# A fused channel-attention and two-FFN kernel: the order of DVE's work in the units of the first pair

## The chip, the cores and the metric

The kernel runs on one core of a Trainium2 chip. The metric is device time in microseconds (us) of one execution. Five engines are named: PE (TensorE, matrix products; its weight loads are shown as PEld), DVE (VectorE, element-wise work), ACT (ScalarE, activations and copies), POOL (GpSimd) and SP (SyncE, which issues transfers). Each engine has its own queue of instructions and works through it in order; semaphores tie the queues together.

## What is computed

The reference, cut to what matters (6016 tokens, 256 channels):

```python
qn = q / (norm(q over tokens) + 1e-6);  kn = k / (norm(k over tokens) + 1e-6)
a = softmax(kn^T @ qn / tau)                  # 256 x 256
x = v @ a                                     # tokens x 256
x = (silu(x @ w_gate) * (x @ w_val)) @ w_out  # 256 -> 1536 -> 256
h = x @ w_in                                  # 256 -> 2048
out = (h * clip(h + 3, 0, 6) / 6) @ w2_out    # 2048 -> 256
```

The five FFN weights arrive as 64-bit floats, and are seen by the kernel as pairs of 32-bit words (a low and a high word).

## The kernel before, in words

Attention is over channels, so its 256x256 matrix is formed once and folded into the first FFN's input weights (w_gate and w_val become a @ w_gate and a @ w_val). The tokens are then taken in pairs of blocks, block 0 and block 1 of 512 tokens each. Every product of two matrices is made as three matmuls, high by high, low weight by high data, high weight by low data: `mm3` (line 96 in the trace, L96).

**Jobs.** A weight block of 128x512 elements is turned from its two words into one float by a `Job`. Its DMA (L109, on SP) brings the raw words into one of two `raw` buffers. `fields()` calls four steps: `cut` on DVE takes out the exponent `e` (L117) and the mantissa bits `m` (L120), `power` on ACT turns `e` into a power of two with two activations (L127, L129), and `mantissa` (L133) and `sign` (L139) on DVE complete `m`. One unit later `scale()` on DVE multiplies the two (L152). For a gate or value block the result goes to `wf`, to be folded; for a block of w_out (a "back weight") ACT's `high()` (L156) copies it rounded into `wo`, and DVE's `low()` (L161) writes the rest.

**The first pair.** The first pair of blocks is worked off in 24 units while the weights are still being converted: one unit for each of 12 slices of 128 hidden channels and each of two blocks (only the last four are in another order). A unit issues, per engine in this order:
- PE: two products of 12 matmuls in all into two PSUM banks (gate first, then value); after units 1, 2, 5, 6, ... 17, 18 a fold of the next weight block (8 matmuls, L628); then the back product (`back`, 6 matmuls into `o`) of the unit whose h was split two units before. The banks b0, b1, a and d are taken in turn by products and folds, and a bank can be written again once its reader is done: Silu for the gate bank, the product on DVE for the value bank, the two copies L705 for a fold's bank.
- ACT: the high part of the last unit's h (L1024), Silu of the gate bank (L1048), `high()` if a w_out block is scaled in this unit, the two `power` activations if there are fields in this unit, and after a fold the two copies of its bank (L705) and the high part of the new weights (L712).
- DVE: the low part of the last unit's h (L1026), low parts of freshly folded weights (L717), `scale()`, the field steps, the product of Silu and value (L1059), `low()`, and what `beside` holds for the unit: sums of the weights (L181 to L184, units 3, 7, 11, 15, 17, 19), the low part of these sums (L717, 128x1024, units 8, 12, 16, 17, 20), and in units 18 to 21 the preparation of the next pair (L337, L340, L349).

The tables `fields` and `scaling` say in which units this happens. Fields: units 0, 1, 2, 4, 5, 6, 8, 9, 10, 12, 13, 14, 16, 17 and 19. Scaling is in the unit after each of these; it is that of a w_out block in units 2, 6, 10, 14, 18 and 20. Units 0, 4, 8, 12, 16 and 19 have fields but no scaling.

After the 24 units the other pairs follow as "cubes", seven products in place of eight (a Strassen scheme), and then the second FFN. The order is written out by hand: within `tc.manual_schedule()` each engine takes the instructions as the program emits them.

Of the kernel before, what the change touches and what calls it, by code (L numbers as in the profile page):

```python
# [18 lines left out]
def channel_attention_then_two_ffns(  # L19
# [71 lines left out]
    def mm3(out, w, x, start, stop):  # L91

        wh, wl = w
        xh, xl = x
        for w, x, first, last in ((wh, xh, start, False), (wl, xh, False, False), (wh, xl, False, stop)):
            nc.tensor.matmul(out, lhsT=w, rhs=x, start=first, stop=last, skip_group_check=True)  # L96
# [136 lines left out]
    jobs, at, second = [], {}, []  # L233
# [32 lines left out]
    passed = [0] * 4  # L266
    limit = [NJ1]

    def load_jobs(ahead=RAW):
        while passed[0] < min(limit[0], passed[1] + ahead):  # L270
            jobs[passed[0]].load()
            passed[0] += 1
# [160 lines left out]
    with tc.manual_schedule():  # L433
# [262 lines left out]
        def fold(m, g):  # L696

            ps = next_bank([P, CT, CW])
            for c in range(CT):
                folding(ps[:, c, :], m, g, c, c == 0)  # L700
            folded.add((m, g))
            fa = FA[g % 2]
            o = CT * m
            for c in range(CT):
                nc.scalar.activation(fa[:, (c, 3 - c)[m]], ps[:, c, :], AF.Copy, scale=rden[:, c : c + 1])  # L705

            w1_hi(g, o, fa[:, o : o + 2])
            return lambda: w1_lo(g, o, fa[:, o : o + 2])
# [27 lines left out]
        def next_bank(shape):  # L736
            tag = ("b0", "b1", "a", "d")[turn[0] % 4]
            turn[0] += 1
            return ps_f.tile(shape, F32, tag=tag, name="ps_" + tag[0])
# [4 lines left out]
        def h_tile(layer):  # L744
            i = counts["h"] = counts["h"] + 1
            if layer == 2 and i % 10 >= 5:
                if i % 10 < 8:
                    return tmp_p.tile([P, TB], F32, tag="m", name="h")
                return e_p.tile([P, TB], F32, tag="e", name="h")
            return h_p.tile([P, TB], F32, tag="h", name="h")  # L750
# [167 lines left out]
        def back():  # L918

            layer, p, block, f, hl = backs.pop(0)  # L920
            t0, n = pairs[p]
            nf = (NF1, NF2)[layer - 1]
            if layer == 1 and p == 0 and f % CT == 0 and block == 0:
                assert passed[3] > at["out", f // CT]
            if f == 0:
                accs[block] = [ps_acc.tile([P, TB], F32, tag=f"acc{CT * block + e}", name="o") for e in range(CT)]
            w = w_of(layer, f)
            for e in range(CT):
                mm3(
                    accs[block][e][:, :n],  # L930
                    (w[:, 0, e * P : (e + 1) * P], w[:, 1, e * P : (e + 1) * P]),
                    (hl[:, 0, :n], hl[:, 1, :n]),
                    f == 0,
                    f == nf - 1,
                )
            if f < nf - 1:
                return
            if (layer, p) not in xr:
                xr[layer, p] = xr_p.tile([P, 2, CT, TB], F32, tag="xr", name="xo")
            x = xr[layer, p]  # L940
            for e in range(CT):
                scale = 1.0 if layer == 1 else 1.0 / 6.0

                if e and p == NP - 1:
                    nc.vector.tensor_scalar(
                        out=x[:, block, e, :n], in0=accs[block][e][:, :n], scalar1=scale, scalar2=None, op0=ALU.mult
                    )
                else:
                    nc.scalar.activation(x[:, block, e, :n], accs[block][e][:, :n], AF.Copy, scale=scale)
                if layer == 1:  # L950
                    nc.sync.dma_start(out=x2_d[p][:, block, e, :n], in_=x[:, block, e, :n])
                else:
                    t = t0 + block * n
                    nc.sync.dma_start(out=outT[e * P : (e + 1) * P, t : t + n], in_=x[:, block, e, :n])
# [30 lines left out]
        fields, scaling, beside = {}, {}, {i: [] for i in U}  # L985
# [35 lines left out]
        def plain_split(between):  # L1021
            f, b, h = h_of
            hl = hl_tile(1)
            nc.scalar.activation(hl[:, 0, :n], h[:, :n], AF.Copy)  # L1024
            between()
            nc.vector.tensor_tensor(out=hl[:, 1, :n], in0=h[:, :n], in1=hl[:, 0, :n].bitcast(F32), op=ALU.subtract)  # L1026
            backs.append((1, 0, b, f, hl))

        for i, (f, b) in enumerate(units):
            w = w_in[1, f // 2][:, f % 2]  # L1030
            pss = []
            for row in ((A11, A12), (S1, A22)):
                ps = next_bank([P, TB])
                for k in range(CT):
                    x = v0[b, k]
                    mm3(
                        ps[:, :n],
                        (w[:, 0, row[k], :], w[:, 1, row[k], :]),
                        (x[:, 0, :n], x[:, 1, :n]),
                        k == 0,  # L1040
                        k == CT - 1,
                    )
                pss.append(ps)

            if h_of:
                plain_split(lambda: None)
            h = h_tile(1)
            nc.scalar.activation(h[:, :n], pss[0][:, :n], AF.Silu)  # L1048
            for go in lows:
                go()  # L1050
            lows = []
            if i in scaling:
                jobs[scaling[i]].scale()
                jobs[scaling[i]].high()
            if i in fields:
                jobs[fields[i]].fields()
                passed[1] += 1
                load_jobs()
            nc.vector.tensor_tensor(out=h[:, :n], in0=h[:, :n], in1=pss[1][:, :n], op=ALU.mult)  # L1059
            h_of = (f, b, h)  # L1060
            if i in scaling:
                jobs[scaling[i]].low()
                passed[2] = passed[3] = scaling[i] + 1
            if i == 10:
                d1, d2, d3, d4, d5, d6 = prep(1)
                for j, step in ((18, d1), (19, d2), (19, d3), (20, d4), (21, d5), (21, d6)):
                    beside[j].append(step)
            for step in beside[i]:
                step()
            g = i // 4 + 1  # L1070
            if i % 4 in (1, 2) and g < NG1:
                m = i % 4 - 1
                assert passed[2] > at[m, g]
                lows.append(fold(m, g))
            while len(backs) > LAG - 1:
                back()
# [5 lines left out]
        for c, key in enumerate(cubes):  # L1082
            layer, p, i = key
# [94 lines left out]
```

## Time and profile before

| what | value |
| --- | --- |
| median of 3 runs | 1103.3 us (1103.25 to 1105.0) |
| the profiled execution | 1105.07 us |
| its span, first to last instruction | 1103.2 us |
| mean granted TensorE clock | 0.999 |
| PE busy | 1090.3 us (99%) |
| PE weight loads busy | 916.2 us (83%) |
| DVE busy | 799.8 us (72%) |
| ACT busy | 760.1 us (69%) |
| POOL busy | 78.2 us (7%) |

The span runs from the first to the last instruction of the profiled execution; its own time is 1.87 us longer. Busy shares are averages over stages with different limits. Matmuls are pipelined and their ends are modelled, so a busy PE is not PE at its peak. In a timeline each row gives the start, the busy time (instructions merged into one row are counted behind the x), the engine, the line, the operation with out<-in, and in brackets the idle time of the engine just before it with what ended it. The busy times of neighbours on one engine overlap a little, so the step from one start to the next is what an operation costs its queue.

### The profile page before, as it was taken

The page shows a single profiled execution, that of the slowest core. Times are in us where ns is not written, and L with a number is a line of the kernel's source. Part 1 is how long each engine was busy: PE and PEld are TensorE (multiplying, and loading weights), DVE is VectorE, ACT ScalarE, POOL GpSimd, SP SyncE. Part 2 cuts the span into 40 slices and gives each one's busy share as a digit, 9 for nine tenths or more (in the row PEclk, how much of TensorE's full clock was granted, in tenths as well). Part 3 has the DMA queues.
Part 4 walks back from the last instruction along what each step waited for, and adds up shares of the span by engine and source line. Part 5 has one row for each costly group of instructions (what it writes and reads, how often), then busy time and mean ns, then how long its engine had stood idle before and what let it go on. Part 6 is the DMA issues. An engine that isn't in the chain of part 4 may idle for free.

```text
span 1103.2 us, 13706 instructions
## 1 busy us (share of the span) xinstructions
PE 1090.3 (99%) x4878; PEld 916.2 (83%) x4878; DVE 799.8 (72%) x1259; ACT 760.1 (69%) x1318; POOL 78.2 (7%) x92
## 2 busy tenths in 40 slices
PE   8989999999999999999999999999999999999998
PEld 6878888888888888888899888888888888888997
DVE  6888996776777677677676677687687687677665
ACT  6666656666766776666766677776766776776765
POOL 0000000111122121211210000000000000000000
PEclk9999999999999999999999999999999999999999
DMA  9523303136337325523665814314324224224100
GB/s 352 211 77 95 115 20 111 62 129 229 110 129 246 132 115 197 199 98 135 225 231 221 330 77 139 128 77 153 115 82 152 111 95 155 89 84 149 40 1 34
DMA packets 56324, 150.31 MB, mean 136 GB/s; under 512 B 5056, under 2 KB 17088, under 8 KB 54848
## 3 DMA queue, kind: packets, MB, share of 16 engines
q1 hardware_dynamic: 55824, 148.92, 37.8%
q8 instruction: 38, 0.62, 0.2%
q10 hardware_dynamic: 432, 0.52, 0.2%
q14 instruction: 30, 0.25, 0.1%
HBM read 89.78 MB, written 59.64 MB: 135 GB/s over the span
## 4 chain that ended last, share of the span: by engine, by line
PE 88%; DVE 6%; ACT 4%; issue 1%; DMA 1%; ACTq 0%; DVEq 0%
PE o L96 38%; PE ps_b L96 20%; PE ps_a L96 13%; PE ps_d L96 13%; PE s L554 4%; DVE hl L1026 1%; DVE w L717 1%; DVE h L1059 1%; ACT w L712 1%; ACT FA L705 1%; ACT hl L1024 1%; DMA tk<-in_k 1%; ACT e L129 1%; ACT e L127 0%; DVE m L133 0%
## 5 line engine op out<-in xcount | busy, mean ns | idle before, releaser
L855 DVE TENSOR_TENSOR hl<-h,hl 128x512 fp32r<-128x512 f32 (+1 forms) x312 | 210.0, 685 | 156.1 <-ACT hl L789 150.8
L96 PE MATMUL o<-hl,w2o 128*128 128x512 f32 (+1 forms) x1152 | 287.6, 385 | 0.0
L96 PEld LDWEIGHTS o<-hl,w2o 128*128 128x128 f32 x1152 | 215.9, 188 | 40.8 <-DVE hl L855 0.6
L789 ACT ACTIVATE hl<-h 128x512 fp32r<-128x512 f32 (+1 forms) x312 | 187.6, 617 | 56.9 <-DVE h L839 52.9
L96 PE MATMUL o<-hl,wo 128*128 128x512 f32 (+1 forms) x864 | 218.1, 387 | 2.1 <-DVE wo L161 1.3
L96 PEld LDWEIGHTS o<-hl,wo 128*128 128x128 f32 x864 | 162.0, 188 | 33.3 <-DVE wo L161 1.7
L96 PE MATMUL ps_b<-op,w 128*128 128x512 f32 (+1 forms) x540 | 139.6, 384 | 0.0
L96 PEld LDWEIGHTS ps_b<-op,w 128*128 128x128 f32 x540 | 101.3, 188 | 18.9 <-ACT ps_b L789 0.4
L96 PE MATMUL ps_b<-op,w2i 128*128 128x512 f32 (+1 forms) x432 | 112.0, 385 | 0.0
L793 DVE TENSOR_TENSOR h<-h,ps_d 128x512 f32<-128x512 f32 (+1 forms) x108 | 72.6, 672 | 52.4 <-PE ps_d L96 47.5
L789 ACT ACTIVATE h<-ps_b 128x512 f32<-128x512 f32 (+1 forms) x108 | 63.4, 587 | 66.7 <-PE ps_b L96 65.7
L789 ACT ACTIVATE ps_b<-ps_a 128x512 f32<-128x512 f32 (+1 forms) x108 | 61.9, 573 | 55.2 <-PE ps_a L96 55.2
L96 PE MATMUL ps_a<-op,w 128*128 128x512 f32 (+1 forms) x360 | 99.4, 384 | 0.0
L96 PE MATMUL ps_d<-op,w 128*128 128x512 f32 (+1 forms) x360 | 99.4, 384 | 0.0
L833 ACT ACTIVATE h<-h,three 128x512 f32<-128x512 f32 (+1 forms) x96 | 68.7, 716 | 40.8 <-DVE h L793 39.5
L96 PEld LDWEIGHTS ps_b<-op,w2i 128*128 128x128 f32 x432 | 81.1, 188 | 15.1
L96 PE MATMUL ps_d<-op,w2i 128*128 128x512 f32 (+1 forms) x288 | 79.8, 385 | 0.1
L793 DVE TENSOR_TENSOR h<-h,ps_b 128x512 f32<-128x512 f32 (+1 forms) x108 | 72.6, 672 | 10.0 <-PE ps_b L96 7.5
L96 PE MATMUL ps_a<-op,w2i 128*128 128x512 f32 (+1 forms) x288 | 79.8, 385 | 0.0
L96 PEld LDWEIGHTS ps_a<-op,w 128*128 128x128 f32 x360 | 67.6, 188 | 12.4
L96 PEld LDWEIGHTS ps_d<-op,w 128*128 128x128 f32 x360 | 67.6, 188 | 12.3
L839 DVE SCALAR_TENSOR_TENSOR h<-h 128x512 f32<-128x512 f32 (+1 forms) x96 | 65.0, 677 | 12.5 <-ACT h L833 12.5
(138 smaller groups left out, 1301.1 us busy)
## 6 DMA issues: line engine op xcount, KB each, us to landing
op<-opd SPq DMA_DIRECT2D x56, 512.0 KB, 4.8
opd<-sp SPq DMA_DIRECT2D x42, 512.0 KB, 2.7
raw<-in_moe_w_out SPq DMA_DIRECT2D x14, 512.0 KB, 4.3
w2i<-wi_d SPq DMA_DIRECT2D x4, 1792.0 KB, 7.4
opd<-st SPq DMA_DIRECT2D x14, 512.0 KB, 2.6
op<-opd SPq DMA_DIRECT2D x14, 448.0 KB, 4.1
tq<-in_q SPq DMA_DIRECT2D x14, 384.0 KB, 7.5
tk<-in_k SPq DMA_DIRECT2D x14, 384.0 KB, 7.5
```

What stands on the lines that cost most here:

```text
L96: nc.tensor.matmul(out, lhsT=w, rhs=x, start=first, stop=last, skip_group_check=True)
L129: nc.scalar.activation(e, e.bitcast(F32), AF.Relu, scale=-1.0, bias=exp_span)
L554: nc.tensor.matmul(s_ps[c], lhsT=tk[:, j - chunks[i][0], c * P : (c + 1) * P], rhs=tq[:, j - chunks[i][0], :], start=(j == 0), stop=(j == ...
L705: nc.scalar.activation(fa[:, (c, 3 - c)[m]], ps[:, c, :], AF.Copy, scale=rden[:, c : c + 1])
L712: nc.scalar.activation(hi, src.rearrange("p o (c f) -> p c o f", c=2), AF.Copy)
L717: nc.vector.tensor_tensor(out=lo, in0=src, in1=hi.bitcast(F32), op=ALU.subtract)
L789: nc.scalar.activation(out[:, : self.n], src[:, : self.n], AF.Copy)
L793: nc.vector.tensor_tensor(out=out[:, :n], in0=a[:, :n], in1=b[:, :n], op=ALU.add)
L833: nc.scalar.activation(r[:, : self.n], x[:, : self.n], AF.Relu, bias=three)
L839: nc.vector.scalar_tensor_tensor(out=r[:, :n], in0=r[:, :n], scalar=6.0, in1=x[:, :n], op0=ALU.min, op1=ALU.mult)
L855: nc.vector.tensor_tensor(out=hl[:, 1, :n], in0=h[:, :n], in1=hl[:, 0, :n].bitcast(F32), op=ALU.subtract)
L1024: nc.scalar.activation(hl[:, 0, :n], h[:, :n], AF.Copy)
```

## The change

In a unit, the block that emits the field steps of a job (with the count that lets the next raw weights be loaded, and that load's issue) stood between `high()` and the product of Silu and value. It now stands behind the product and behind `low()`. Nothing else is changed.

```diff
             if i in scaling:
                 jobs[scaling[i]].scale()
                 jobs[scaling[i]].high()
-            if i in fields:
-                jobs[fields[i]].fields()
-                passed[1] += 1
-                load_jobs()
+
             nc.vector.tensor_tensor(out=h[:, :n], in0=h[:, :n], in1=pss[1][:, :n], op=ALU.mult)
             h_of = (f, b, h)
             if i in scaling:
                 jobs[scaling[i]].low()
                 passed[2] = passed[3] = scaling[i] + 1
+            if i in fields:
+                jobs[fields[i]].fields()
+                passed[1] += 1
+                load_jobs()
             if i == 10:
                 d1, d2, d3, d4, d5, d6 = prep(1)
```

## Rows read from the trace of the kernel before

**Rows 1.** The page, part 1: busy time, share of the span, instructions.
```profile
PE 1090.3 (99%) x4878; PEld 916.2 (83%) x4878; DVE 799.8 (72%) x1259; ACT 760.1 (69%) x1318; POOL 78.2 (7%) x92
```
**Rows 2.** The page, part 4: the chain that ended last, by engine.
```profile
PE 88%; DVE 6%; ACT 4%; issue 1%; DMA 1%; ACTq 0%; DVEq 0%
```
**Rows 3.** Windows: busy PE, PEld, DVE, ACT, POOL; PEclk, DMA share, GB/s.
```profile
100.00:110.00 10.00, 10.00 (x46) 8.42 (x45) 8.79 (x15) 6.18 (x11) 0.00 (x0) 1.00 0.37 105
```
**Rows 4.** Timeline of PE in the first pair.
```profile
69.03 1.99 PE L628 MATMUL ps_d<-wf_x,early 128*128 128x256 f32 x8 [1.42 <-DVE h L1059]
...
75.31 1.43 PE L96 MATMUL o<-hl,wo 128*128 128x512 f32 x5 [1.31 <-DVE wo L161]
...
86.48 1.52 PE L96 MATMUL ps_d<-v,w 128*128 128x512 f32 x6
...
106.28 1.52 PE L96 MATMUL ps_b<-v,w 128*128 128x512 f32 x6
...
166.66 1.52 PE L96 MATMUL o<-hl,wo 128*128 128x512 f32 x6
168.29 3.01 PE L96 MATMUL ps_b<-v,w 128*128 128x512 f32 x12
```
**Rows 5.** Timeline of DVE, units 0, 9, 10 and 18.
```profile
61.44 0.42 DVE L117 TENSOR_SCALAR e<-raw 128x512 uint32<-128x512 uint32 x1
...
63.57 0.69 DVE L1059 TENSOR_TENSOR h<-h,ps_b 128x512 f32<-128x512 f32 x1
...
103.20 0.68 DVE L1026 TENSOR_TENSOR hl<-h,hl 128x512 fp32r<-128x512 f32 x1
...
104.41 0.42 DVE L117 TENSOR_SCALAR e<-raw 128x512 uint32<-128x512 uint32 x1
...
108.29 0.69 DVE L1026 TENSOR_TENSOR hl<-h,hl 128x512 fp32r<-128x512 f32 x1 [1.07 <-ACT hl L1024]
...
109.50 0.69 DVE L152 TENSOR_TENSOR m<-m,e 128x512 f32<-128x512 f32 x1
110.10 0.42 DVE L117 TENSOR_SCALAR e<-raw 128x512 uint32<-128x512 uint32 x1
...
114.16 0.69 DVE L1026 TENSOR_TENSOR hl<-h,hl 128x512 fp32r<-128x512 f32 x1 [0.65 <-ACT hl L1024]
...
150.13 0.68 DVE L1059 TENSOR_TENSOR h<-h,ps_a 128x512 f32<-128x512 f32 x1
150.91 0.69 DVE L161 TENSOR_TENSOR wo<-m,wo 128x512 fp32r<-128x512 f32 x1
```
**Rows 6.** Timeline of ACT, units 0, 6, 9 and 10.
```profile
64.29 0.63 ACT L1024 ACTIVATE hl<-h 128x512 fp32r<-128x512 f32 x1 [0.91 <-DVE h L1059]
...
88.34 0.61 ACT L1024 ACTIVATE hl<-h 128x512 fp32r<-128x512 f32 x1
...
104.86 0.73 ACT L127 ACTIVATE e<-e,exp_top 128x512 f32<-128x512 uint32 x1 [1.56 <-DVE e L117]
...
106.25 0.82 ACT L705 ACTIVATE FA<-ps_b,rden 128x256 f32<-128x256 f32 x2
...
107.64 0.61 ACT L1024 ACTIVATE hl<-h 128x512 fp32r<-128x512 f32 x1
...
110.22 0.63 ACT L156 ACTIVATE wo<-m 128x512 fp32r<-128x512 f32 x1 [1.48 <-DVE m L152]
110.75 0.71 ACT L127 ACTIVATE e<-e,exp_top 128x512 f32<-128x512 uint32 x1
...
113.51 0.61 ACT L1024 ACTIVATE hl<-h 128x512 fp32r<-128x512 f32 x1
```
**Rows 7.** Transfers of the raw weights in the first pair, issue to landing.
```profile
DMA to landing us min/median/max: 3.4/3.7/3.8
```
**Rows 8.** Waits of ACT, 60 to 180 us: total, times, longest.
```profile
ACT h L1048 <- PE ps_b L96: 1.5, 2, 0.9
...
ACT h L1048 <- PE ps_a L96: 0.6, 2, 0.4
```

## The prediction, made before the changed kernel was run

> **What bounds the kernel now.** I read the page first. TensorE shows as busy for 99% of the span [rows 1] and carries 88% of the chain that ended last [rows 2]. That is an average, and the change touches one stage only, the first pair, whose 24 units run from about 57 to 175 us (their first matmul and the last L1026). So I read the windows of that stage next: in a typical one PE is busy without a gap and DVE is at 8.79 of 10 us [rows 3]. PE looks like the bound there too, until its timeline is read for waits. PE waits three times: 1.42 us for the product of unit 1, which frees bank d; 1.31 us for the low part of w_out; and at 168.29 us, where six matmuls begun at 166.66 at 1.36 us per six should have let the next ones start at 168.02: 0.27 us late [rows 4]. The last wait matters most: at the end of the stage PE stands directly behind DVE and ACT. Whatever delays their chain by then is added to the end.
>
> That chain is seen by laying the DVE timeline [rows 5] beside the ACT one [rows 6]. Take the h of unit 8. Its L1026 starts on DVE at 103.20, the cut at 104.41, ACT's exponent at 104.86, the two fold copies at 106.25, the L1024 of unit 9 at 107.64, and DVE's next L1026 at 108.29 after 1.07 us idle. ACT is in order, so the exponents (L127, L129) stand ahead of the fold copies, of the weights' high part and of the next L1024; and L127 waits for the cut. **The cut is therefore on the chain, while the product is not.** From one L1024 (unit 5, 88.34) to the one four units later (unit 9, 107.64) this chain takes 19.30 us [rows 6]; PE's four units, from 86.48 to 106.28, take 19.80 us [rows 4]. The chain has 0.50 us per four units to spare, no more.
>
> **The change, part by part.** It adds and removes no instruction. On DVE, in the 15 units with fields, the four field operations go behind the product; in units 2, 6, 10 and 14, which also split a back weight, behind that low part too. ACT's order stays, as neither moved operation has a part there, but L127 now waits for a later cut.
>
> *Product ahead of the cut.* A 512-column DVE operation holds the next one back 0.60 us (scale at 109.50, cut at 110.10 [rows 5]). In units 1, 5, 9 and 13 (scale, fields, then a fold) the cut lies on the chain with nothing beside it: +0.60 each, so 2.40 us.
>
> *Low part ahead of the cut too.* In unit 10 the scale is at 109.50 and ACT's high part at 110.22; L127 follows at 110.75, held by ACT's own order, not by the cut at 110.10. With the new order the product is at 110.10. The low part waits for the high one; what that costs is seen in unit 18, which has no fields: product 150.13, low part 150.91, 0.78 us later [rows 5]. So low at 110.88, cut 0.60 later at 111.48, L127 0.45 behind it (104.41 to 104.86) at 111.93 instead of 110.75: +1.18. Four such units: 4.72 us. What queues behind the new wait is the four field operations; what is late next is ACT's fold copies, the weights' high part, the next h's L1024, and through it the next unit's L1026 and L717, for whose result the second product of the next weight block waits on PE.
>
> *Units with fields and no scale.* Here the product was on the chain. In unit 0 it comes at 63.57, behind a cut at 61.44, and L1024 at 64.29 waits for it. Afterwards: product 61.44, cut 62.04, L127 62.49; two exponents take 1.39 us (104.86 to 106.25), so L1024 starts at 63.88, a gain of 0.41. The same in unit 4. In units 8, 12 and 16 DVE has the low parts of the weight sums between product and L1026, so that L1026 does not wait for ACT (103.20 shows no idle time [rows 5]): the same operations in another order, nothing. The sum: 2 x -0.41 = -0.82.
>
> *Edits costed at nothing.* Units 3, 7, 11, 15, 18 and 20 to 23 have no fields, and their order stays. In 17 and 19 DVE is full with weight sums up to the next L1026, in any order; uncovered, unit 17 would cost 0.60. The load of the next raw weights is issued on SP behind the fields, up to 1.2 us later. It lands in 3.7 us [rows 7], and its cut comes two units on, half of 19.80 us later; without that cover DVE would stand still for up to those 3.7 us. POOL's queue has nothing in this stage.
>
> *The PE waits.* PE does gain early: bank d comes free sooner and its first wait goes. But the early lead is spent where PE next needs weights that are 1.18 us late, because order on PE is fixed too. I count it at nothing, since the end of the stage goes by the chain.
>
> **Sum:** 2.40 + 4.72 - 0.82 = 6.30 us. The profiled execution took 1105.07 us (its span is 1103.2; 1.87 us lie around it), which gives 1111.37 for it. The median of the runs shown, 1103.3, is 1.77 us below that execution, so I forecast **1109.6 us**. The chain then needs 19.30 + 0.60 + 1.18 = 21.08 us per four units against PE's 19.80, and nothing catches it up. In the later stages PE has the work and DVE is less loaded; the delay is kept to the end.
>
> *Bounds.* ACT's Silu waits for PE 2.1 us in this stage (1.5 and 0.6 [rows 8]); if all of that were cover for the chain, and the 0.41 came in all five units (-2.05), the sum would be 2.40 + 4.72 - 2.05 - 2.1 = 2.97. I take those waits as no cover, since each is followed by a longer wait of L127 for the cut. Upwards, no gain from unit 0's kind and unit 17 added: 3.00 + 4.72 = 7.72.
>
> **Rivals.** (a) *Faster.* The early product ends PE's waits. Place: bank d at 69.03, the w_out part at 75.31, and 168.29. Price: 1.42 + 1.31 + 0.27 = 3.0 us, so 1100.3. It decides if the exponents have 1.2 us of room on ACT ahead of the folds. For it: PE's two largest waits are on the two operations moved forward. Against it: ACT is released by the cut at 104.86 and runs from there to 107.64 into an L1024 that DVE waits for [rows 5, 6]. The Trainium skill, Perfetto Trace Analysis, section Optimization Strategy, speaks for this case: find the gaps of the engine that is to be sped up and make the dependencies behind them start sooner. The trace agrees as to the gaps, not as to the price paid elsewhere.
> (b) *Same.* PE hides it: no instruction is added, and the chain's extra stays under PE's time. That needs an extra of at most 0.50 us per four units, where I find 1.78; then 1103.3. The same page, section Identifying the Most-Contended Engine, advises working on the engine with the highest occupancy, though it calls matmul busy time a bad measure for TensorE. By that rule a reordering on DVE would not show here. The chance of it also covers the change not taking effect, but the rows of before follow the written order on each engine.
> (c) *Much slower.* Each operation ahead of a cut counts in full, in all 15 units, with the 0.58 (1.18 less 0.60) in four: 9.0 + 2.3 = 11.3 us, so 1114.6. Against it: DVE is full in units 8, 12, 16, 17 and 19, where order alone costs nothing.
>
> **How the numbers follow.** Forecast 0.86; (a) 0.04; (b) 0.04; (c) 0.06. About 0.2%, 2.2 us, is what a measurement of this kernel can tell from no change. Slower is the forecast and (c): 0.92; same 0.04; faster 0.04. The range takes the lower bound, 1103.3 + 2.97 = 1106.3, and the upper one, 1103.3 + 7.72 = 1111.0, with the 1.75 us by which the runs of before differ (1103.25 to 1105.0) on top: 1112.8. It leaves out (a), (b) and (c), 0.14.
>
> **What the next profile would show.** Right: in units 1, 2, 5, 6, 9, 10, 13 and 14 DVE's idle time ahead of L1026 grows from 1.07 and 0.65 to about 1.7; four units take the L1024 chain about 21.1 us; PE waits about 1 us for L717 in the second product of units 4, 8, 12 and 16; cube 0's first product starts about 6.3 us later and the rest keeps that distance; busy times and clock stay. Wrong: if L127 starts no later behind the preceding L1024 than now, or PE's four units still take 19.80 us, the chain was not the limit. If only the w_out units are longer, the 0.60 term is wrong; if units 8, 12 and 16 grow too, (c) is nearer.

## The result, and the profile after

The changed kernel takes 1109.82 us (median of 6 runs, 1108.73 to 1111.6) against 1103.56 us for the kernel before (6 runs beside them): a ratio of 1.0061, 95% interval 1.005 to 1.0071, so 5.5 to 7.8 us slower. The forecast was 1109.6.

| what | before | after |
| --- | --- | --- |
| profiled execution, its span | 1105.07, 1103.2 us | 1108.73, 1106.9 us |
| PE, DVE, ACT busy | 1090.3, 799.8, 760.1 us | 1090.0, 800.3, 759.6 us |
| mean granted clock | 0.999 | 0.999 |
| first gate product of unit 1 on PE | 60.27 us | 57.44 us |
| first product of cube 0 on PE | 172.50 us | 176.24 us |
| the stage between the two | 112.23 us | 118.80 us |

The two spans differ by 3.7 us only, because the attention part in front of the stage, which the change does not touch, came out 2.83 us shorter in the execution profiled after (57.44 against 60.27). The stage itself is 6.57 us longer, and from cube 0's first product to the end of the span both take 930.7 us. In the other profiles below the stage starts between 58.1 and 60.2 us, so all of them are read from unit 1's first gate product on.

The same engines are as busy as before; the page cannot show the cause. The timeline of PE of the changed kernel, rows with a wait of the stage (as in [rows 4]):

```profile
70.01 0.50 PE L96 MATMUL o<-hl,wo 128*128 128x512 f32 x1 [0.45 <-ACT wo L156]
70.73 1.43 PE L96 MATMUL o<-hl,wo 128*128 128x512 f32 x5 [0.22 <-DVE wo L161]
...
73.97 0.50 PE L96 MATMUL ps_d<-v,w 128*128 128x512 f32 x1 [0.45 <-ACT w L712]
75.82 1.42 PE L96 MATMUL ps_d<-v,w 128*128 128x512 f32 x5 [1.34 <-DVE w L717]
...
96.16 1.43 PE L96 MATMUL ps_b<-v,w 128*128 128x512 f32 x5 [0.24 <-DVE w L717]
...
117.26 1.43 PE L96 MATMUL ps_d<-v,w 128*128 128x512 f32 x5 [1.01 <-DVE w L717]
...
138.37 1.43 PE L96 MATMUL ps_b<-v,w 128*128 128x512 f32 x5 [1.01 <-DVE w L717]
...
158.95 1.43 PE L96 MATMUL ps_d<-v,w 128*128 128x512 f32 x5 [0.44 <-DVE w L717]
...
168.08 1.67 PE L96 MATMUL ps_d<-v,w 128*128 128x512 f32 x6 [0.88 <-DVE h L1056]
...
172.02 3.02 PE L96 MATMUL ps_b<-v,w 128*128 128x512 f32 x12 [0.89 <-ACT h L1048]
```

Of the two longest waits that PE had, the 1.42 us for bank d are gone, and the 1.31 us for the w_out block are down to 0.45 for its high part and 0.22 for its low part. In their place PE now waits for folded weights in every fourth unit (their low part, L717, once after a wait for their high part, L712), and twice for a bank at the end. The cause lies one engine further back. DVE, units 9 and 10 of the changed kernel (L1056 is the product):

```profile
104.35 0.68 DVE L1056 TENSOR_TENSOR h<-h,ps_d 128x512 f32<-128x512 f32 x1
104.95 0.42 DVE L117 TENSOR_SCALAR e<-raw 128x512 uint32<-128x512 uint32 x1
...
108.82 0.69 DVE L1026 TENSOR_TENSOR hl<-h,hl 128x512 fp32r<-128x512 f32 x1 [1.67 <-ACT hl L1024]
...
110.03 0.69 DVE L152 TENSOR_TENSOR m<-m,e 128x512 f32<-128x512 f32 x1
110.64 0.68 DVE L1056 TENSOR_TENSOR h<-h,ps_a 128x512 f32<-128x512 f32 x1
111.42 0.69 DVE L161 TENSOR_TENSOR wo<-m,wo 128x512 fp32r<-128x512 f32 x1
112.03 0.42 DVE L117 TENSOR_SCALAR e<-raw 128x512 uint32<-128x512 uint32 x1
...
115.91 0.69 DVE L1026 TENSOR_TENSOR hl<-h,hl 128x512 fp32r<-128x512 f32 x1 [1.67 <-ACT hl L1024]
```

and ACT beside it:

```profile
87.08 0.61 ACT L1024 ACTIVATE hl<-h 128x512 fp32r<-128x512 f32 x1
...
105.40 0.72 ACT L127 ACTIVATE e<-e,exp_top 128x512 f32<-128x512 uint32 x1 [2.58 <-DVE e L117]
...
108.18 0.61 ACT L1024 ACTIVATE hl<-h 128x512 fp32r<-128x512 f32 x1
...
110.75 0.63 ACT L156 ACTIVATE wo<-m 128x512 fp32r<-128x512 f32 x1 [1.48 <-DVE m L152]
112.48 0.73 ACT L127 ACTIVATE e<-e,exp_top 128x512 f32<-128x512 uint32 x1 [1.10 <-DVE e L117]
...
115.26 0.61 ACT L1024 ACTIVATE hl<-h 128x512 fp32r<-128x512 f32 x1
```

L127 waits 2.58 us for its cut where it waited 1.56 [rows 6], and in unit 10 it waits 1.10 us where it followed the high part at once. DVE then stands idle 1.67 us ahead of L1026, in place of 1.07 and 0.65 [rows 5] (1.66 or 1.67 us in each of the units 1, 2, 5, 6, 9, 10, 13 and 14, as foretold). DVE has come by the product early and has nothing else to do while ACT catches up. From the L1024 of unit 5 (87.08) to that of unit 9 (108.18) it is 21.10 us, against 19.30 before; the prediction had 21.08.

### The profile page after: what moved, and what is told of

The parts are those of the page before. It is cut to its first block, busy times and chain, and to the rows that moved or that the text cites. A ratio compares the mean times of both kernels' runs of the same rounds, so it can differ in the third digit from the quotient of the medians.

```text
span 1106.9 us, 13706 instructions
## 1 busy us (share of the span) xinstructions
PE 1090.0 (98%) x4878; PEld 913.9 (83%) x4878; DVE 800.3 (72%) x1259; ACT 759.6 (69%) x1318; POOL 78.2 (7%) x92
## 4 chain that ended last, share of the span: by engine, by line
PE 88%; DVE 6%; ACT 4%; issue 1%; DMA 1%; ACTq 0%; DVEq 0%
PE o L96 38%; PE ps_b L96 20%; PE ps_a L96 13%; PE ps_d L96 13%; PE s L554 3%; DVE w L717 1%; DVE h L1056 1%; ACT e L127 1%; ACT e L129 1%; ACT w L712 1%; ACT hl L1024 1%; ACT FA L705 1%; DMA tk<-in_k 1%; DVE hl L1026 0%; DVE e L117 0%
```

## The experiments

Each profile was read in one way. For every unit, the start of its L1024 on ACT is taken from that run's timeline, less the start of unit 1's first gate product on PE. The table gives the difference to the kernel before; the last line is the same for cube 0's first product on PE.

| after unit | changed | product alone | low alone | cuts stay | cuts first | units 0, 4.. | units 1, 5.. | units 2, 6.. |
| --- | --- | --- | --- | --- | --- | --- | --- | --- |
| 0 | -0.40 | -0.40 | 0.00 | -1.00 | -1.00 | -0.40 | 0.00 | +0.01 |
| 1 | +0.19 | +0.18 | 0.00 | -0.90 | -2.11 | -0.42 | +0.60 | +0.01 |
| 2 | +1.39 | +0.60 | +1.21 | -0.90 | -2.89 | -0.42 | +0.60 | +1.22 |
| 5 | +1.57 | +1.16 | +1.21 | -1.82 | -4.94 | -0.83 | +1.19 | +1.20 |
| 6 | +2.77 | +1.57 | +2.41 | -1.81 | -5.00 | -0.84 | +1.18 | +2.40 |
| 9 | +3.37 | +2.42 | +2.41 | -1.94 | -4.44 | -0.39 | +1.78 | +2.40 |
| 10 | +4.58 | +2.84 | +3.62 | -1.92 | -4.49 | -0.39 | +1.79 | +3.61 |
| 13 | +5.17 | +3.43 | +3.61 | -1.94 | -3.94 | +0.11 | +2.38 | +3.60 |
| 14 | +6.39 | +3.85 | +4.82 | -1.94 | -3.99 | +0.11 | +2.39 | +4.81 |
| 23 | +6.57 | +4.01 | +5.07 | -1.68 | -4.00 | +0.78 | +2.37 | +4.80 |
| cube 0 | +6.57 | +4.01 | +6.58 | -1.66 | -3.71 | +0.79 | +2.39 | +4.82 |

**Product alone.** The low part stays behind the fields.

```diff
-            if i in fields:
-                jobs[fields[i]].fields()
-                passed[1] += 1
-                load_jobs()
             nc.vector.tensor_tensor(out=h[:, :n], in0=h[:, :n], in1=pss[1][:, :n], op=ALU.mult)
             h_of = (f, b, h)
+            if i in fields:
+                jobs[fields[i]].fields()
+                passed[1] += 1
+                load_jobs()
             if i in scaling:
                 jobs[scaling[i]].low()
```

> Product alone ahead of the fields, low part behind them as before. Chain theory (what counts is how much later the exponent cut L117 comes, since ACT's exponents stand ahead of the fold copies and of L1024): +0.60 in units 1, 5, 9, 13; in units 2, 6, 10, 14 L127 was held 0.65 behind the cut by the high part, of which 0.20 is more than the link needs, so only +0.40 there; -0.41 in units 0 and 4: 2.40 + 1.60 - 0.82 = +3.2 us against the kernel before. Rival (it is the product that blocks: DVE stands still for Silu or for PE's bank with the fields queued behind it): all of the loss is already here, +6 us.

Measured: 1108.39 us against 1103.97, ratio 1.0033 (1.002 to 1.0046), 2.2 to 5.1 us; the stage 4.01 us longer. The chain theory's 3.2 lies inside, the rival's 6 does not. In unit 10 L127 comes 0.40 us later behind its L1024 than before (111.48 - 107.97 = 3.51, before 3.11), as expected. The stage's excess over 3.2 lies elsewhere: the 0.41 of unit 4 does not come (+0.61 after unit 3, +0.58 after unit 4), from unit 7 to unit 9 it is 0.85 in place of 0.60, and behind unit 14 another 0.16 comes, as 0.18 does in the changed kernel. The first two have one cause, which the DVE timeline of this run shows in units 4 and 8 (L1055 is the product):

```profile
79.27 0.69 DVE L1055 TENSOR_TENSOR h<-h,ps_d 128x512 f32<-128x512 f32 x1 [0.29 <-PE ps_d L96]
...
99.07 0.69 DVE L1055 TENSOR_TENSOR h<-h,ps_b 128x512 f32<-128x512 f32 x1 [0.17 <-PE ps_b L96]
```

The product waits there for PE's bank, with the fields queued behind it; in the kernel before and in the changed kernel no product of this stage waits for PE. PE was late there, as it had lost 1.6 us at a lower clock (told below). Without that loss, by these rows, both banks would have been ready ahead of the product; so some 0.6 of the 4.01 us belong to this execution and not to the order.

**Low part alone.** In units 2, 6, 10 and 14 it stands ahead of fields and product.

```diff
+            if i in scaling:
+                jobs[scaling[i]].low()
+                passed[2] = passed[3] = scaling[i] + 1
             if i in fields:
...
             nc.vector.tensor_tensor(out=h[:, :n], in0=h[:, :n], in1=pss[1][:, :n], op=ALU.mult)
             h_of = (f, b, h)
-            if i in scaling:
-                jobs[scaling[i]].low()
-                passed[2] = passed[3] = scaling[i] + 1
```

> Low part of the back weight alone ahead of the fields, product behind them as before. Chain theory: only units 2, 6, 10, 14 change; the scale-to-low step is 1.38 and the cut follows 0.60 later, so L127 comes 1.2 us later in each: +4.8 us. Rival (the product blocks): only the 0.2 us that DVE waits for the high part in four units, +0.8 us or less.

Measured: 1108.38 us, ratio 1.0038 (1.0025 to 1.005), 2.8 to 5.5 us. The steps in the table are 1.21, 1.20, 1.21 and 1.20, in these four units alone: the chain theory's, and far over the rival's 0.8 in all. They are as long as those of the changed kernel, where the product stands ahead of the cut as well: from scale to low part it is 1.38 us here in unit 10 (109.75 to 111.13) and 1.39 there (110.03 to 111.42), since the product fills the time in which the low part waits for the high one. (The same edit puts the low part ahead of the product in units 18 and 20 too; unit 20 adds 0.24.) The 6.58 us on PE in this one profile hold 1.5 us of a lower clock, told below.

**The cuts stay.** L117 and L120 keep their place; mantissa and sign go behind product and low part.

```diff
             if i in fields:
-                jobs[fields[i]].fields()
-                passed[1] += 1
-                load_jobs()
+                jobs[fields[i]].cut()
+                jobs[fields[i]].power()
...
                 jobs[scaling[i]].low()
                 passed[2] = passed[3] = scaling[i] + 1
+            if i in fields:
+                jobs[fields[i]].mantissa()
+                jobs[fields[i]].sign()
+                passed[1] += 1
+                load_jobs()
```

> Product and low part ahead of mantissa and sign only; the two cut operations (L117, L120) stay where they were ahead of the product. Chain theory: the exponents start as early as before, the product is 1.3 us earlier, units 0 and 4 no longer wait for it: -1 to -2 us against the kernel before (1.5 by adding the links up unit by unit). Rival (the product blocks): DVE still reaches mantissa and sign behind the product and the low part, so most of the loss stays, +4 us or more.

Measured: 1101.99 us (11 runs), ratio 0.9982 (0.9973 to 0.9991): faster than the kernel before, by 1.0 to 3.0 us. The product stands directly behind the cuts, and the loss is gone. What remains of PE's waits in the stage, timeline of PE:

```profile
72.53 1.42 PE L96 MATMUL o<-hl,wo 128*128 128x512 f32 x5 [0.64 <-DVE wo L161]
75.93 1.43 PE L96 MATMUL ps_d<-v,w 128*128 128x512 f32 x5 [0.39 <-DVE w L717]
```

**The cuts first.** They go to the head of the unit, and ACT's exponents ahead of the high part of the back weight.

```diff
+            if i in fields:
+                jobs[fields[i]].cut()
             if h_of:
                 plain_split(lambda: None)
...
                 jobs[scaling[i]].scale()
+            if i in fields:
+                jobs[fields[i]].power()
+            if i in scaling:
                 jobs[scaling[i]].high()
```

(product, low part, mantissa, sign and load follow as in the run with the cuts left in place)

> The cut operations go to the head of the unit, ahead of L1026, and ACT's two exponents ahead of the high part of the back weight; product and low part ahead of mantissa and sign. Chain theory: ACT need not wait for DVE between Silu and the fold copies, the chain of four units falls below PE's 19.80 us, and PE's three waits of the stage (3.0 us by their idle times, 3.7 with the weight loads behind them) go: -3 to -3.7 us, faster than both kernels. Rival (the product blocks): +4 us or more as in the run with the cuts left in place.

Measured: 1100.73 us against 1103.97, ratio 0.9965 (0.9953 to 0.9978), 2.4 to 5.2 us faster than the kernel before and faster than both kernels of this study. The stage is 3.71 us shorter. Its ACT timeline in units 9 and 10 shows an engine whose longest waits are for PE in place of DVE (L1050 is Silu):

```profile
101.76 0.84 ACT L705 ACTIVATE FA<-ps_b,rden 128x256 f32<-128x256 f32 x2 [0.73 <-PE ps_b L628]
...
104.50 0.60 ACT L1050 ACTIVATE h<-ps_b 128x512 f32<-128x512 f32 x1 [0.71 <-PE ps_b L96]
104.99 0.71 ACT L127 ACTIVATE e<-e,exp_top 128x512 f32<-128x512 uint32 x1
105.74 0.72 ACT L129 ACTIVATE e<-e,exp_span 128x512 uint32<-128x512 f32 x1
106.37 0.61 ACT L156 ACTIVATE wo<-m 128x512 fp32r<-128x512 f32 x1
107.58 0.84 ACT L705 ACTIVATE FA<-ps_d,rden 128x256 f32<-128x256 f32 x2 [0.60 <-PE ps_d L628]
```

PE's timeline has no wait from the first unit to cube 0. The windows of 55 to 175 us, first the kernel before, then this one, show PE's busy time (first figure with a count) go from 117.02 to 119.85 of 120 us:

```profile
55.00:175.00 120.00, 117.02 (x517) 96.43 (x515) 105.83 (x191) 77.02 (x135) 0.00 (x0) 1.00 0.23 71
```

```profile
55.00:175.00 120.00, 119.85 (x533) 99.73 (x532) 106.24 (x192) 81.36 (x142) 0.00 (x0) 1.00 0.24 74
```

**One instruction taken back.** The changed kernel, with the exponent cut alone ahead of the product: `cut(both=False)` emits L117 and `cut_m` L120.

```diff
+            if i in fields:
+                jobs[fields[i]].cut(both=False)
+                jobs[fields[i]].power()
             nc.vector.tensor_tensor(out=h[:, :n], in0=h[:, :n], in1=pss[1][:, :n], op=ALU.mult)
...
             if i in fields:
-                jobs[fields[i]].fields()
+                jobs[fields[i]].cut_m()
+                jobs[fields[i]].mantissa()
+                jobs[fields[i]].sign()
```

> The changed order, with one instruction taken back: the exponent cut L117 (0.42 us) alone stays ahead of the product and the low part; L120, mantissa and sign stay behind them. Chain theory: the wait that counts is ACT's for L117 and nothing else, so the whole loss of 6.3 us goes and a little is gained by the earlier product: -1.3 us against the kernel before, -7.5 against the changed one; the L1024 of each unit about 0.8 (unit 2) to 1.5 us (unit 6) earlier than before. Rival (the field operations as a whole are missed, or the product blocks DVE): the kernel stays within 1.5 us of the changed one, +4.5 to +6.

Measured: 1102.45 us (12 runs) against 1104.18, ratio 0.9991 (0.9982 to 1.0): 0 to 2 us faster than before, where the changed kernel is 5.5 to 7.8 slower. The stage is 0.85 us shorter (111.38), and the high parts of h (there L1029) of units 2 and 6 come 0.78 and 1.58 us earlier. The 0.85 us are less than the 1.3 expected: at unit 12 some 0.6 us are given back, where the product waits 0.51 us for PE's bank d (116.44 in that run's DVE timeline). The load of the next raw weights stands behind product and low part here as in the changed kernel, so it is not what costs the time. It is the place of this one 0.42 us instruction that makes the loss.

**One kind of unit at a time.** The changed order in units with `i % 4` equal to 0 (in the second run 1, in the third 2), the old order in all others.

```diff
+            if i % 4 == 0:
...
+            else:
...
```

> The changed order in units 0, 4, 8, 12 and 16 only, where there are fields and no scale. Theory as predicted (-0.41 in units 0 and 4, nothing elsewhere): L1024 of the later units 0.8 us earlier than before. A finer version of it: early units gain 0.4 each, but in units 8, 12 and 16, where DVE is no longer behind PE, the product ahead of the fields makes DVE stand still for PE's value bank, and up to 0.7 each is given back: +0.4 at the end of the stage.

> The changed order in units 1, 5, 9, 13 and 17 only. Theory: +0.60 at each of units 1, 5, 9 and 13, nothing at 17, so +2.4 us at the end of the stage. Rival (PE's longer period covers the first 0.50 us of every four units): +0.4 us.

> The changed order in units 2, 6, 10 and 14 only. Theory: +1.2 us at each, +4.8 at the end of the stage (predicted 4.72). Rival (PE's longer period covers the first 0.50 us of every four units): +2.8 us.

Measured, one execution each (1104.96, 1107.05 and 1109.19 us; single times move with the start of the stage, so the table decides): +0.79, +2.39 and +4.82 us at cube 0. The second and third are additive to a few hundredths: 4 x 0.60 and 4 x 1.20. The rival that PE covers the first 0.50 us of four units falls. The first is neither of the two expected values, and nearer to the finer one: -0.40 in units 0 and 4 as predicted, but later units give it back. There DVE has caught up with PE, and the product, now ahead of the fields, stops the queue for PE's bank. DVE timeline of that run, unit 16:

```profile
137.71 0.69 DVE L1056 TENSOR_TENSOR h<-h,ps_b 128x512 f32<-128x512 f32 x1 [0.41 <-PE ps_b L96]
138.31 0.42 DVE L117 TENSOR_SCALAR e<-raw 128x512 uint32<-128x512 uint32 x1
```

## Why the prediction was right

**Product ahead of the cut, 4 x 0.60 = 2.40.** Measured 2.37 to 2.39 with these units alone.

**Low part ahead of the cut, 4 x 1.18 = 4.72.** Measured 4.80 to 4.82 alone, and the steps in the changed kernel are 1.20, 1.20, 1.21 and 1.22. The price of the low part's wait, taken from unit 18 (0.78 us behind the product), holds: 110.64 to 111.42.

**Units with fields and no scale, 2 x -0.41 = -0.82.** The two gains came at -0.40 each. Mis-sized is the zero set for units 8, 12 and 16: alone, they turn the gain into a loss of 0.79. In the changed kernel, where the chain runs late and no product waits for PE, the zero holds in units 8 and 12; behind unit 14 another 0.18 us is lost (+6.39 to +6.57), which neither of the other two kinds loses there. Together that is -0.63 for this kind, and the others leave the same: 6.57 - 2.38 - 4.81 = -0.62.

**Sum.** 6.30 predicted, 6.57 in the stage, 6.3 in the medians. The terms are right to a few tenths of a microsecond. That the time itself came out within 0.2 us of the forecast is in part luck, as the six executions spread over 2.9 us.

**PE's early lead counted at nothing.** PE's first wait went (bank d at 64.62 in sequence, no wait), and the lead ended at 75.82 on L717, as said. The waits of about 1 us for L717 came in units 4, 12 and 16 (1.34, 1.01, 1.01); in unit 8 it was 0.24, as the four units up to it hold the gain of unit 4 and take 20.34 us (75.82 to 96.16) in place of 21.1. The last two waits, 0.88 and 0.89 us, show that PE waits for the chain at the end of the stage.

**What was wrong in the reasoning.** The prediction gave the chain 0.50 us of room per four units and made this the point from which rival (b) decides. There was no such room: units 1, 5, 9 and 13 alone add 0.60 to 19.30, a tenth of a microsecond over PE's 19.80, and the whole 2.4 us come out. Before the change the L1024 chain runs at 19.30 from unit 5 to unit 17 (28.07, 47.37, 66.67 and 85.96 us in the measure of the table): PE never held it back (no product on DVE waits for PE there), so nothing of it was cover. A difference of two periods is room only once the slower one has become the limit.

**The rivals.** (a), a faster kernel by the early product, needs the cut to stay early: the two runs that keep both cuts ahead of the product are faster. The Trainium skill, Perfetto Trace Analysis, section Optimization Strategy, says to find the gaps of the engine that is to be sped up and to make the dependencies behind them start sooner. The trace agrees for these two runs: PE's waits fall to 1.03 us with the cuts left in place and to none with the cuts first. The dependency to start sooner was the exponents', not the product's. (b) is outside the interval. (c) would be 11.3 us, outside it as well.

## What to carry to other kernels

On an engine that is not the bound (DVE is 72% busy over the span, 105.83 of 120 us in this stage) and has an in-order queue, the order decides by what another engine's queue waits for: put first the short instruction that releases a long chain elsewhere (here a 0.42 us cut ahead of two exponents, two fold copies and a split), and let work whose result is needed a unit later fill the gap. When an operation is moved up, look first at what it is moved past, and follow who waits for that. And read the room of a chain from waits that it shows, not from a difference of averages.

## What the runs showed of the hardware

After a wait PE can lose time a second time, to a lower clock. In the profile of the low part alone, PE waited 2.28 us for a bank at 168.39, and a little over a microsecond after it went on, the granted clock fell to 0.50, the lower of its two levels (1.2 GHz), for about three microseconds. Windows of that profile, PEclk third from the end:

```profile
168.00:169.00 1.00, 0.61 (x3) 0.52 (x4) 1.00 (x2) 0.00 (x0) 0.00 (x0) 1.00 0.00 0
169.00:170.00 1.00, 1.00 (x6) 0.79 (x5) 1.00 (x2) 0.49 (x1) 0.00 (x0) 0.91 0.00 0
170.00:171.00 1.00, 1.00 (x4) 0.81 (x3) 0.90 (x3) 1.00 (x3) 0.00 (x0) 0.50 0.00 0
171.00:172.00 1.00, 1.00 (x3) 0.77 (x3) 1.00 (x3) 1.00 (x3) 0.00 (x0) 0.50 0.00 0
172.00:173.00 1.00, 1.00 (x4) 0.76 (x3) 1.00 (x3) 1.00 (x3) 0.00 (x0) 0.50 0.00 0
173.00:174.00 1.00, 1.00 (x6) 0.82 (x5) 1.00 (x3) 0.70 (x2) 0.00 (x0) 0.88 0.09 16
```

Six matmuls that take 1.36 us at full clock took 2.56 there (169.91 to 172.47), the next twelve 3.09 in place of 2.72: 1.57 us in all, close to the 1.51 us by which PE's 6.58 us exceed the chain's 5.07 in that run. With the product alone a wait of 2.16 us was followed by the same fall early in the stage. PE's timeline there:

```profile
73.41 1.43 PE L96 MATMUL o<-hl,wo 128*128 128x512 f32 x5 [2.16 <-DVE wo L161]
74.67 2.63 PE L96 MATMUL ps_a<-v,w 128*128 128x512 f32 x6
77.09 2.07 PE L96 MATMUL ps_d<-v,w 128*128 128x512 f32 x6
79.00 1.52 PE L96 MATMUL o<-hl,wo 128*128 128x512 f32 x6
```

The twelve matmuls from 74.67 to 79.00 took 4.33 us in place of 2.72, so PE lost 1.61 us, and its late banks held the products of units 4 and 8 up. With units 1, 5, 9 and 13 alone a wait of 2.16 us was followed by no fall. The waits of the kernel before, 1.42 us at most, were followed by none either. What decides whether the clock falls was not tested.
